# A linear-attention and SwiGLU kernel: y and the state update move ahead of the weight work in steps 6 to 11

## The chip, the cores and the metric

The kernel runs on one core of a Trainium2 chip. The metric is the device time of one execution in microseconds (us). A second figure is the span of one profiled execution, from the first to the last instruction; all times inside the kernel are counted from the start of that span.

The engines are called by short names: PE does matrix products (PEld is its weight load), ACT, DVE and POOL are three elementwise engines, and SP issues most of the DMA transfers. Each runs its own list of instructions in the order in which the program writes them, and they wait for one another through semaphores.

## The reference

The first half is an attention with a decaying state; its output becomes the input rows of a gated feed-forward block.

```python
# r, k, v: (4, 8, 768, 48); w, u: (8, 48)
for t in range(S):
    cur = einsum('bhd,bhe->bhde', u * k[t], v[t])
    y[t] = einsum('bhd,bhde->bhe', r[t], state + cur)
    state = w * state + einsum('bhd,bhe->bhde', k[t], v[t])
# x: y as (4*768, 8*48) = (3072, 384)
g = x @ w_gate                      # (384, 1536)
out = (g * sigmoid(g) * (x @ w_val)) @ w_out      # (3072, 384)
```

## The kernel before

The 768 time steps are cut into 6 chunks of 128, and with 4 batches this makes 24 units; unit i is chunk i // 4 of batch i % 4. Inside a unit the recurrence is done with matrix products: k and r are scaled by powers of w, `turn` transposes them on PE into PSUM tiles `tp`, from which ACT copies them to kT and rT (L341, L345). `scores` (L373) multiplies kT by rT into two tiles `s_ps`, and DVE's copy_predicated puts the part above the diagonal into At. `outputs` (L389) makes y of the unit: At times v and, from the second chunk on, the batch's state Z times rT, into `y_ps`, which ACT copies to xT. `update` (L415) multiplies k by v into `u_ps`; DVE adds it to Z and POOL scales Z by w.

The feed-forward work is cut into small pieces in a list `todo`, taken by `feed`. A piece of the first kind is `gate_value` (L442): twelve matmuls of 256 columns into one tile `gv`, a sigmoid on ACT and two products on DVE. Later pieces are products of a Strassen-like scheme (`four`, `project`). With a piece, `feed(1, 3)` also takes up to three ACT products that write the diagonal of At (L320). The weights come as 64-bit numbers and are rounded to 32 bits in 18 pieces by `round_weights`: three ACT passes (`w_mag` and `w_low`, L173 and L179), four DVE passes (L188, L189) and a POOL add (L216), which belongs to the piece before. After the 18 pieces the same places in the program hold four POOL subtractions of output weights (`weight_sum`).

The program's order is the engines' order: the schedule is written by hand. One loop over s (L804) runs the steps. A step s prepares unit s + 1 (POOL products, DMA loads on SP), turns unit s, does the scores of unit s - 1, and the y and state of unit s - 2. Between these stand five gaps. In steps 5 to 11 the dictionary EARLY says what a gap holds: F is a feed, R is a call of round_weights. For steps 7 to 11 the five gaps hold R, F, R, F and RF; for steps 5 and 6 the first one is empty. From step 12 on, k and r are turned by DMA and DVE instead of PE, and the gaps hold an even share of the list.

The PSUM pool `ps_a` has four buffers used in rotation. A step below 12 asks for six tiles: two `tp`, two `s_ps`, one `y_ps`, one `u_ps`. The tile `gv` has a pool of its own with two buffers.

The lines that place y and the state in the step are these:

```python
            scores(s - 1)
            if s >= LATE:
                outputs(s - 2)
                update(s - 2)
            gaps(s, 1)
...
        gaps(s, 2)
        if s - 2 >= 4 and (s < LATE or s > N):
            outputs(s - 2)
            update(s - 2)
```

Of the kernel before, what the change touches and what calls it, by code (L numbers as in the profile page):

```python
# [22 lines left out]
def fast(  # L23
# [349 lines left out]
    def scores(i):  # L373

        ps = [ps_a.tile([P, HP, P], FP32, name="s_ps", tag="a") for _ in range(2)]
        for a in range(HP):
            for e in range(2):
                rows = slice(64 * e, 64 * e + D)
                pe.matmul(  # L379
                    ps[e][:, a, :], kT[i % 2][rows, at(i, a), :], turned[i][rows, at(i, a), :],  # L380
                    start=True, stop=True, skip_group_check=True,
                )
        for e in range(2):
            dve.copy_predicated(  # L384
                At[i % 2][:].rearrange("p (a e) t -> p a e t", e=2)[:, :, e],
                mask[:].bitcast(INT32).unsqueeze(1).to_broadcast([P, HP, P]), ps[e][:],
            )

    def outputs(i):  # L389

        c, b = divmod(i, B)
        A, vl, z = At[i % 2], v_ld[i % 4], Z[b]
        rT = turned.pop(i)
        ps = ps_a.tile([P, CC, P], FP32, name="y_ps", tag="a")
        cols = [[] for _ in range(4)]
        for m in range(4 * CC):
            (cc, q), (a, s) = divmod(m, 4), divmod(m, 3)
            each = [(z[0:R2, a, 32 * s : 32 * s + 32], rT[0:R2, at(i, a), :])] if c > 0 else []  # L400
            if s < 2:
                each.append((vl[:, a, 32 * s : 32 * s + 32], A[:, 2 * a, :]))
            if s > 0:
                each.append((vl[:, a, 32 * s + 16 : 32 * s + 48], A[:, 2 * a + 1, :]))
            cols[q] += [(cc, x, n == 0, n == len(each) - 1) for n, x in enumerate(each)]
        for n in range(len(cols[0])):
            for q in range(4):
                cc, x, start, stop = cols[q][n]
                pe.matmul(  # L409
                    ps[32 * q : 32 * q + 32, cc, :], *x,  # L410
                    start=start, stop=stop, skip_group_check=True,
                )
        act.copy(xT[:, i % NX, :, :], ps[:])  # L413
# [287 lines left out]
    def gaps(s, n):  # L701

        if s not in EARLY:
            if n == 0:
                share[0] = min(-(-len(todo) // (4 - (s - 9) % 4)), 14)
            feed(share[0] // 5 + (n < share[0] % 5))
            return
        for what in EARLY[s][n]:
            if what == "R":
                if done["pool"] < NW:  # L710
                    round_weights()
                elif len(summed) < 4:
                    weight_sum()
            else:
                feed(1, 3)

    share = [0]
    BLOCKS = 12
    LATE = 12
    EARLY = {s: ("" if s < 7 else "R", "F", "R", "F", "RF") for s in range(5, 12)}  # L720
    EARLY[4] = ("R", "F", "", "F", "F")

# [81 lines left out]
    for s in range(4, N + 2):  # L804
# [11 lines left out]
        if 4 <= s - 1 < N:  # L816
            while small:
                small.popleft()()
# [3 lines that stand above are left out]
# [6 lines left out]
# [3 lines that stand above are left out]
# [22 lines left out]
@with_exitstack  # L853
def kernel(
    ctx: ExitStack,
    tc: tile.TileContext,
    *args: bass.AP,
):
    nc = tc.nc
    ctx.enter_context(tc.manual_schedule())  # L860
    flag = ctx.enter_context(tc.tile_pool(name="flag", bufs=1))
    outside = flag.tile([1, 1], INT32, name="outside")
    fast(tc, *args, outside[:])
    n = nc.values_load(outside[:], min_val=0, max_val=512)
    with tc.If(n > 0):
        general(tc, *args)
# [397 lines left out]
```

## Time and profile before

| what | value |
|---|---|
| device time, median of 3 runs | 625.29 us (624.53 to 626.14) |
| span of the profiled execution | 623.3 us |
| PE busy | 611.0 us, 98% |
| DVE, ACT, POOL busy | 358.6, 238.9, 296.9 us |
| step 6, from its y to the next: PE, DVE, ACT, POOL busy of 12.15 us | 12.15, 10.90, 11.50, 10.15 us |
| one gv group of six matmuls inside a run, start to start | about 1.3 us |
| y_ps of a unit, then u_ps, start to start | 1.56 and 0.45 us |
| granted PE clock | 0.999 |

A busy share is an average over a whole span or window. The matmuls overlap one another, so the distance between the starts of two groups says more of their cost than the duration that a line gives. An idle time is shown with the releaser, the instruction whose end let the waiting one go.

### The profile page before, as it was taken

How to read it: one execution, taken by the hardware profiler on the slowest of the kernel's cores; microseconds unless marked ns; L12 is line 12 of the kernel's file. 1: busy time of each engine (PE TensorE's matmuls, PEld its weight loads, DVE VectorE, ACT ScalarE, POOL GpSimd, SP SyncE). 2: the span in 40 equal slices, each digit the busy share in tenths (PEclk: the TensorE clock that was granted, in tenths of full speed). 3: DMA queues.
4: the chain of work that ended last, by engine and by line, in shares of the span. 5: the costliest groups of instructions: out<-in, count | busy, mean ns of one | idle time of the engine just before them, and what ended most of it. 6: DMA issues, size and time to landing. Idle time of an engine off the chain costs nothing.

```text
span 623.3 us, 13014 instructions
## 1 busy us (share of the span) xinstructions
PE 611.0 (98%) x5040; PEld 552.1 (89%) x5040; DVE 358.6 (58%) x751; ACT 238.9 (38%) x647; POOL 296.9 (48%) x350
## 2 busy tenths in 40 slices
PE   8799999999999999999999999999999999999996
PEld 7688888899888899888899888899988899988896
DVE  6888997373566574466575355574354463355460
ACT  3368785312444412344331335422243321233310
POOL 4789789935556315364452636341334211443110
PEclk9999999999999999999999999999999999999999
DMA  7989873233232213322223312221000000000001
GB/s 187 218 215 252 260 242 65 50 62 82 57 60 34 40 16 76 65 42 46 44 34 70 78 16 32 31 41 38 26 1 2 2 0 26 26 1 2 1 2 56
DMA packets 138008, 40.47 MB, mean 65 GB/s; under 512 B 128592, under 2 KB 131792, under 8 KB 137936
## 3 DMA queue, kind: packets, MB, share of 16 engines
q1 hardware_dynamic: 134480, 34.82, 26.4%
q10 hardware_dynamic: 3456, 4.72, 2.1%
q8 instruction: 42, 0.69, 0.5%
q14 instruction: 30, 0.25, 0.1%
HBM read 28.51 MB, written 4.72 MB: 53 GB/s over the span
## 4 chain that ended last, share of the span: by engine, by line
PE 90%; POOL 2%; DMA 1%; ACT 1%; DVE 1%; issue 0%; SPq 0%; ACTq 0%; POOLq 0%
PE c_b L625 25%; PE c_a L625 21%; PE o_f L519 13%; PE o_a L519 8%; PE gv L448 7%; PE o_b L519 6%; PE y_ps L409 5%; PE s_ps L379 3%; PE u_ps L424 1%; PE tp L341 1%; DMA r_ld<-in_r_dram 1%; POOL wg L216 1%; POOL wv L216 1%; POOL rk L228 0%; POOL hats L299 0%
## 5 line engine op out<-in xcount | busy, mean ns | idle before, releaser
L609 POOL TENSOR_TENSOR hT<-hT,u 128x256 f32<-128x256 f32 x60 | 47.0, 785 | 148.7 <-DVE hT L608 121.6
L632 ACT COPY u<-c_a 128x256 f32<-128x256 f32 x120 | 44.5, 371 | 85.8 <-PE c_a L625 83.3
L625 PE MATMUL c_a<-t,wv 128*128 128x256 f32 x240 | 72.1, 382 | 0.1
L625 PE MATMUL c_b<-xT,wg 128*128 128x256 f32 x240 | 71.7, 380 | 0.0
L605 ACT ACTIVATE sg<-hT 128x256 f32<-128x256 f32 x120 | 50.0, 416 | 52.5 <-DVE hT L634 33.8
L320 ACT ACTIVATE At<-ident,du 128x128 f32<-128x128 f32 x176 | 62.0, 398 | 16.0 <-DVE o_sb L533 7.2
L625 PE MATMUL c_b<-xT,s 128*128 128x256 f32 x240 | 61.7, 380 | 0.0
L639 DVE TENSOR_TENSOR u<-u,c_b 128x256 f32<-128x256 f32 x60 | 25.1, 419 | 60.5 <-PE c_b L625 55.4
L625 PEld LDWEIGHTS c_a<-t,wv 128*128 128x128 f32 x240 | 45.0, 190 | 6.8 <-ACT u L632 1.2
L625 PEld LDWEIGHTS c_b<-xT,s 128*128 128x128 f32 x240 | 45.3, 190 | 6.5
L625 PEld LDWEIGHTS c_b<-xT,wg 128*128 128x128 f32 x240 | 45.4, 190 | 5.9
L634 DVE TENSOR_TENSOR hT<-p,c_b 128x256 f32<-128x256 f32 x60 | 25.2, 420 | 41.7 <-PE c_b L625 39.1
L585 POOL TENSOR_TENSOR s<-wv,wg 128x256 f32<-128x256 f32 x24 | 17.6, 734 | 65.5 <-PE o_f L519 50.8
L384 DVE COPY_PREDICATED At<-mask,s_ps 128x512 f32<-128x512 int32 x48 | 33.0, 741 | 21.3 <-PE s_ps L379 12.4
L302 POOL TENSOR_TENSOR hats<-r_ld,rscale 128x384 f32<-128x384 f32 x20 | 20.8, 1040 | 35.3 <-DMA hats<-hats 25.2
L448 PE MATMUL gv<-xT,wg 128*128 128x256 f32 x144 | 36.7, 391 | 0.6 <-ACT xT L413 0.6
L637 DVE TENSOR_TENSOR hT<-hT,c_a 128x256 f32<-128x256 f32 x60 | 25.3, 421 | 19.5 <-PE c_a L625 18.3
L641 DVE TENSOR_TENSOR hT<-u,c_b 128x256 f32<-128x256 f32 x60 | 25.2, 421 | 19.4 <-PE c_b L625 19.2
L625 PE MATMUL c_b<-t,s 128*128 128x256 f32 x120 | 36.2, 383 | 0.0
L409 PE MATMUL y_ps<-At,v_ld 128*32 128x128 f32 x768 | 34.9, 273 | 1.3 <-DVE At L384 1.3
L625 PE MATMUL c_b<-xT,wv 128*128 128x256 f32 x120 | 35.9, 381 | 0.0
L625 PE MATMUL c_a<-t,s 128*128 128x256 f32 x120 | 35.8, 380 | 0.0
(135 smaller groups left out, 1384.3 us busy)
## 6 DMA issues: line engine op xcount, KB each, us to landing
hats<-hats SPq DMA_DIRECT2D x192, 32.0 KB, 2.0
w_bits<-in_moe_w_gate_dram SPq DMA_DIRECT2D x6, 768.0 KB, 6.4
v_ld<-in_v_dram SPq DMA_DIRECT2D x48, 96.0 KB, 3.3
w_bits<-in_moe_w_val_dram SPq DMA_DIRECT2D x6, 768.0 KB, 6.3
w_bits<-in_moe_w_out_dram SPq DMA_DIRECT2D x6, 768.0 KB, 6.7
out_dram<-o_sb ACTq DMA_DIRECT2D x24, 192.0 KB, 1.9
k_ld<-in_k_dram SPq DMA_DIRECT2D x20, 192.0 KB, 3.1
r_ld<-in_r_dram SPq DMA_DIRECT2D x20, 192.0 KB, 3.8
```

Source lines behind the costliest of these rows:

```text
L320: lambda h=h: act.activation(At[i % 2][:, h, :], ident[:], AF.Identity, scale=du[:, h : h + 1])
L384: dve.copy_predicated(At[i % 2][:].rearrange("p (a e) t -> p a e t", e=2)[:, :, e], mask[:].bitcast(INT32).unsqueeze(1).to_broadcast([P, H ...
L409: pe.matmul(ps[32 * q : 32 * q + 32, cc, :], *x, start=start, stop=stop, skip_group_check=True,)
L448: pe.matmul(gv[:, o, :].rearrange("p (i t) -> p i t", i=2), wt[:, c, P * f : P * (f + 1)], xT[:, 2 * g % NX : 2 * g % NX + 2, c, :], start ...
L519: pe.matmul(ps, lhs[:, f, :], rhs[:, f, :], start=(f == 0 and n in (0, 1, 4)), stop=(f == FH - 1), skip_group_check=True,)
L605: act.activation(x[what, f][:], h[j], AF.Sigmoid)
L609: pool.tensor_mul(h[1], h[1], x.pop(("u3", f))[:])
L625: pe.matmul(ps.rearrange("p (i t) -> p i t", i=2), lhs, rhs, start=first, stop=what not in ("p2", "p5", "p4", "p3"), skip_group_check=True,)
L632: act.copy(x[nm, f][:], ps)
L634: dve.tensor_add(h[0], x.pop(("p1", f))[:], ps)
L637: dve.tensor_mul(h[0], h[0], ps)
L641: dve.tensor_add(h[1], x.pop(("u2", f))[:], ps)
```

## The change

One constant goes from 12 to 6. In steps 6 to 11, `outputs(s - 2)` and `update(s - 2)` no longer stand behind the second and third gap (F and R), but directly behind `scores(s - 1)`. These are the units 4 to 9. On PE this means: scores, y, u and then three gate_value pieces in a row, where there was one gate_value piece between scores and y and two behind u. The xT copy on ACT, the Z additions on DVE and the Z products on POOL move with it. In step 11 the block of DMAs that begins to turn unit 12 stands behind y and u instead of ahead of them. Steps 4, 5 and those from 12 on are as they were.

```diff
     share = [0]
     BLOCKS = 12
-    LATE = 12
+    LATE = 6
     EARLY = {s: ("" if s < 7 else "R", "F", "R", "F", "RF") for s in range(5, 12)}
```

## The prediction

> **What bounds the kernel now.** I read the page first: the share of each engine, then the chain that ended last, then the timelines of PE, ACT, POOL and DVE over the six steps that the change touches (s = 6 to 11, about 53 to 131 us).
>
> ```profile
> PE 611.0 (98%) x5040; PEld 552.1 (89%) x5040; DVE 358.6 (58%) x751; ACT 238.9 (38%) x647; POOL 296.9 (48%) x350
> ```
>
> PE is busy nearly everywhere, but shares are averages. In the windows by step, the first touched step reads (span, then busy time of PE, PEld, DVE, ACT, POOL):
>
> ```profile
> 57.76:69.91 12.15, 12.15 (x149) 10.56 (x149) 10.90 (x24) 11.50 (x29) 10.15 (x10) 1.00 0.87 257
> ```
>
> PE has no hole in those 12.15 us, yet ACT, DVE and POOL are at 95%, 90% and 84%: they still round weights (calls R: three ACT passes, four DVE passes, one POOL add each). The four steps from 69.91 to 118.50 also show PE full, and from 131 to 600 us the windows have 468.8 of 468.9 us busy. So what PE loses or wins in steps 6 to 11 should reach the end undiminished.
>
> The chain of waits in order of time (start, length, what) says how step 6 was reached:
>
> ```profile
> 52.90 1.80 POOL wv L216
> 54.70 0.02 issue
> 54.73 0.93 ACT w_low L179
> 55.65 0.41 ACT w_mag L173
> 56.06 0.30 ACT sg L454
> 56.37 0.87 ACT At L320 x3
> 57.24 0.48 ACT kT L345
> 57.72 0.04 issue
> 57.76 1.75 PE y_ps L409 x56
> ```
>
> Here y of unit 4 waited for ACT's copy kT of unit 6. Not for its contents: the pool ps_a has four PSUM buffers in rotation, and a step asks for six (two tp, two s_ps, y_ps, u_ps), so y_ps always gets the buffer of the first tp of the same step, and that copy empties it. The copy was late because ACT had waited on a POOL add to reuse w_low. In PE's timeline (start, duration) that wait hardly shows:
>
> ```profile
> 54.61 1.56 PE L448 MATMUL gv<-xT,wg 128*128 128x256 f32 x6
> 56.01 1.46 PE L448 MATMUL gv<-xT,wv 128*128 128x256 f32 x6
> 57.76 0.43 PE L409 MATMUL y_ps<-rT,Z 112*32 112x128 f32 x8 [0.29 <-ACT kT L345]
> ```
>
> PE spent almost the whole delay on a gate_value call (F) that stands between scores and y. This is the point of the case.
>
> A step in steady state, PE's timeline of step 8:
>
> ```profile
> 79.27 1.56 PE L448 MATMUL gv<-xT,wg 128*128 128x256 f32 x6
> 80.67 1.46 PE L448 MATMUL gv<-xT,wv 128*128 128x256 f32 x6
> 82.06 0.43 PE L409 MATMUL y_ps<-rT,Z 112*32 112x128 f32 x8
> ...
> 83.62 0.52 PE L424 MATMUL u_ps<-v_ld,hats 128*32 128x48 f32 x32
> 84.07 1.56 PE L448 MATMUL gv<-xT,wg 128*128 128x256 f32 x6
> 85.47 1.46 PE L448 MATMUL gv<-xT,wv 128*128 128x256 f32 x6
> 86.77 1.46 PE L448 MATMUL gv<-xT,wg 128*128 128x256 f32 x6
> 88.06 1.46 PE L448 MATMUL gv<-xT,wv 128*128 128x256 f32 x6
> 89.36 0.82 PE L341 MATMUL tp<-ident,hats 128*128 128x128 f32 x6
> ```
>
> From start to start: a group of six gv matmuls inside a run takes 1.295 us, the first after smaller tiles 1.40, the last ahead of y_ps 1.39. So the lone F costs 2.79 and the two together 5.29.
>
> [...] nothing from behind y_ps ran in the 0.36 us hole at 57.40. So a matmul put ahead of an F holds the F back. [...] the granted clock is 1.00 throughout. [...] The trace shows one such buffer wait, the 0.29 us above.
>
> **The change part by part.** No instruction is added or removed. In each of steps 6 to 11 the 56 matmuls of y, the 32 of u, ACT's xT copy, DVE's two Z adds and POOL's two Z products move ahead of F, R (and F's sigmoid and two products). No DMA is issued by what moves.
>
> *Junctions on PE, a gain.* F now stands with the two others: 1.40 + 5 x 1.295 = 7.88 us against 2.79 + 5.29 = 8.08, so 0.20 less a step, 1.2 in six. Scores to y costs what scores to F does: step 12 has that order already, and there s_ps to y_ps starts 131.10 and 132.19, 1.09 us, as at 78.18 to 79.27. PE's own step becomes 0.97 (tp) + 1.09 + 1.56 + 0.45 + 7.88 = 11.95 against 12.15.
>
> *Step 6, the loss.* All that leads to kT at 57.72 lies ahead of the moved code, so y stays at 57.76. Scores end at 54.61. PE now idles 3.15 us, and F, which filled 2.79 of it, comes after u (59.78). Three F end at 59.78 + 7.88 = 67.66, where the turn of unit 7 started at 65.06: 2.59 later. This is net of the first 0.20.
>
> *Steps 7 and 8, the new bound.* y must follow kT of its own step. Behind the second F, ACT has in order: its sigmoid, three At, R (1.76), the third sigmoid, three At, kT. In step 6 that ran from 62.47 (end of gv) to 67.24, 4.77 us, plus 0.06 to y: 4.83. PE itself needs from the same point 2.59 (third F) + 0.97 + 1.09 = 4.65. So each y waits 0.18: second F ends at 65.06, y at 69.89; then 7.30 to the next second F's end and 4.83 again, 12.13 a step: y at 82.02 and 94.15.
>
> *Steps 9 to 11.* The last R of step 9 has only a POOL add, since all 18 pieces have been through ACT. ACT then needs some 2.0 us from the third F's end to kT against PE's 2.06: no wait, 11.95 each. y at 106.10 and 118.05; u ends at 120.06, two F at 125.35, where the projection's first o_a started at 123.21 before. The sum is **+2.14 us**.
>
> *The other queues.* ACT: xT's copy ahead of the sigmoid waits for y's end, but the five At products that precede it end at 59.67 and y at 59.33, so about nothing; R behind it starts 2.8 us later in step 6 because the sigmoid it follows waits for the later F, and this is what the 4.77 already holds. DVE: Z's adds stand behind the copy_predicated that ended at 60.79, when u is done, so they run about 2 us earlier; F's products and R queue behind 0.73 us. POOL: Z's product goes ahead of an R add; worked through, POOL's add of R ends at about 78.2 in step 7 and the ACT pass that reuses its buffer is due at 79.1, a margin of 0.9. PSUM of F: the third F needs the first F's products, done 1.1 us ahead. SP: loads of v wait for u, which ends at the same times as before to a few tenths; loads of k and r wait for POOL's own product, about 1 us later with a step in hand; step 11's block-moving DMAs read nothing that moved. I count these at nothing; what hides them is PE's 12 us step, and POOL works a step ahead of PE. In steps 7 and 8 the bounds are 0 (ACT comes earlier) and 1 us each (R waits on POOL or DVE); from both sides, 0.4 below and 1.6 above the sum. The 3.15 us at step 6 is bounded too: the copy hangs on a DMA of r that landed at 46.88 and a full POOL[...].
>
> **The rivals.**
> 1. *The filled wait opens and is never recovered* (forecast). 625.29 + 2.14 = 627.4; own range 626.6 to 628.4. Chance 0.52, of which 0.04 stays within the bound.
> 2. *The copy is earlier than in this one execution.* The page shows one; if kT comes 1 us sooner, step 6 loses 1.6, and the total is +1.1, 626.4. For it: the start depends on DMA; against: the three runs lie within 1.6 us. Chance 0.22, mostly no change.
> 3. *Not slower: PE's junctions decide.* If ACT's kT of step 6 is done when scores end, six gains of 0.20 remain: 624.1. It decides as soon as the copy comes before 54.7, three microseconds earlier than in the trace; what speaks for it is only that from step 7 on kT is within 0.2 us of being in time. Chance 0.10, a third of it over the bound, if more than the junctions comes free.
> 4. *ACT, DVE or POOL fall further behind.* They are 84 to 95% busy in step 6. If R waits 1 us more in steps 7 and 8[...], the total is about +3.8: 629.1. Chance 0.16.
> That the change does nothing is excluded: the order is written out by hand, and units 4 to 9 are all moved.
>
> **How the numbers follow.** The profile's own span would go from 623.3 to 625.4; the runs (624.53 to 626.14) lie 1 to 3 us above that span, so I add the sum to their median: 627.4. The bound for no change is 0.3%, 1.9 us, about what a measurement of this kernel can tell. From the cases: slower by more 0.67, within 0.30, faster 0.03. The range reaches down to case 2 with kT 1.9 us sooner and up past the middle of case 4: 625.5 to 629.5.
>
> **What would show it right or wrong.** In the changed profile y_ps of step 6 should carry about 3 us of idle time released by kT, at about 57.8; the y_ps of steps 7 and 8 some 0.2 each, those of 9 to 11 none; three F in a row of 7.9 us; steps of 12.1, then 11.95; the first o_a about 2.1 us later, and no difference after it. Wrong would be: y_ps of step 6 before 56, waits on kT of over 0.5 in later steps, a PE clock below 1, or a different length of what follows 125 us.

## The result and the profile after

The changed kernel takes 628.92 us (median of 6 runs, 628.20 to 630.11) against 625.50 us before (6 runs, 624.53 to 626.14): 1.0057 times the time before, 95% interval 1.0043 to 1.0071, so 3.4 us slower. A second set of runs on another chip gave 629.93 against 625.65, again 1.0057 (1.0041 to 1.0074); the medians themselves lie 4.3 us apart there. The prediction was 627.4, range 625.5 to 629.5, slower with a chance of 0.67.

The page of the changed kernel shows almost the same PE work in a longer span (628.4 us, 623.3 before):

```profile
PE 612.8 (98%) x5040; PEld 554.0 (88%) x5040; DVE 356.9 (57%) x751; ACT 238.7 (38%) x647; POOL 296.3 (47%) x350
```

The windows from y to y (span, busy time of PE, PEld, DVE, ACT, POOL, then the granted PE clock) say where the time went. Steps 6, 7, 9 and 10:

```profile
57.43:72.21 14.78, 14.66 (x148) 12.76 (x149) 9.14 (x20) 9.05 (x24) 9.13 (x9) 0.81 0.81 226
72.21:84.34 12.13, 12.02 (x148) 10.61 (x148) 11.15 (x24) 9.83 (x24) 10.35 (x10) 1.00 0.80 238
...
96.48:108.43 11.95, 11.95 (x148) 10.62 (x148) 9.74 (x21) 8.32 (x21) 10.17 (x10) 1.00 0.33 63
108.43:120.38 11.95, 11.95 (x150) 10.62 (x148) 5.11 (x11) 4.92 (x15) 11.64 (x9) 1.00 0.28 51
```

Steps 7, 9 and 10 take 12.13, 11.95 and 11.95 us, as forecast. Step 6 takes 14.78, and its clock is 0.81: the profile before had 1.00 there.

The chain of waits that leads to y of step 6 is nearly the old one, and y starts at nearly the old time, 57.43 (57.76 before):

```profile
52.60 1.79 POOL wv L216
54.40 0.02 issue
54.42 0.91 ACT w_low L179
55.33 0.40 ACT w_mag L173
55.73 0.30 ACT sg L454
56.04 0.87 ACT At L320 x3
56.91 0.48 ACT kT L345
57.39 0.04 issue
57.43 0.63 PE y_ps L409 x5
```

What changed is what PE does meanwhile. Its timeline of step 6, from the scores to the next turn:

```profile
53.21 1.16 PE L379 MATMUL s_ps<-rT,kT 48*128 48x128 f32 x16
57.43 0.65 PE L409 MATMUL y_ps<-rT,Z 112*32 112x128 f32 x8 [3.06 <-ACT kT L345]
...
60.42 0.87 PE L424 MATMUL u_ps<-v_ld,hats 128*32 128x48 f32 x32
61.22 2.44 PE L448 MATMUL gv<-xT,wg 128*128 128x256 f32 x6
63.49 1.46 PE L448 MATMUL gv<-xT,wv 128*128 128x256 f32 x6
...
69.97 1.04 PE L341 MATMUL tp<-ident,hats 128*128 128x128 f32 x8
```

PE waits 3.06 us for the copy that it waited 0.29 for before, since the F that lay between is now behind. The first matmuls after the hole are slow: y to u takes 2.99 us (1.56 before), u to F 0.80 (0.45), the first gv group 2.27 (1.40), together 2.65 us too long. The windows of one microsecond show why; the granted clock is the third number from the end:

```profile
55.00:56.00 1.00, 0.00 (x0) 0.00 (x0) 0.49 (x2) 1.00 (x4) 1.00 (x1) 1.00 0.91 168
56.00:57.00 1.00, 0.00 (x0) 0.00 (x0) 0.96 (x3) 1.00 (x5) 1.00 (x2) 0.60 0.95 328
57.00:58.00 1.00, 0.57 (x12) 0.54 (x16) 0.96 (x3) 1.00 (x3) 1.00 (x2) 0.50 1.05 381
...
62.00:63.00 1.00, 1.00 (x4) 0.82 (x3) 0.12 (x1) 0.00 (x0) 0.85 (x3) 0.50 1.14 197
63.00:64.00 1.00, 1.00 (x6) 0.84 (x5) 0.00 (x0) 0.00 (x0) 1.00 (x1) 0.99 0.79 156
```

A mean of 0.60 in the second window puts the fall to half at 56.2, some 1.8 us after the scores' last matmul had ended (54.4); full speed is back at 63.0. From then on everything is a shift: the first o_a, where the gates end, starts at 127.68 (123.21 before), and from there to the end it takes 500.7 us (500.1 before).

### The profile page after: what moved, and what is told of

Read it like the earlier page. It is cut to its first block, busy times and chain, and to the rows that moved or that the text cites. A ratio compares the mean times of both kernels' runs of the same rounds, so it can differ in the third digit from the quotient of the medians.

```text
span 628.4 us, 13007 instructions
## 1 busy us (share of the span) xinstructions
PE 612.8 (98%) x5040; PEld 554.0 (88%) x5040; DVE 356.9 (57%) x751; ACT 238.7 (38%) x647; POOL 296.3 (47%) x350
## 4 chain that ended last, share of the span: by engine, by line
PE 86%; POOL 3%; ACT 3%; DVE 2%; issue 1%; ACTq 0%; POOLq 0%
PE c_b L625 25%; PE c_a L625 20%; PE o_f L519 13%; PE o_a L519 8%; PE o_b L519 6%; PE y_ps L409 6%; PE gv L448 5%; PE s_ps L379 3%; PE u_ps L424 1%; ACT At L320 1%; POOL wv L216 1%; ACT w_low L179 1%; ACT w_mag L173 0%; POOL hats L299 0%; POOL rk L228 0%
## 5 line engine op out<-in xcount | busy, mean ns | idle before, releaser
L409 PE MATMUL y_ps<-At,v_ld 128*32 128x128 f32 x768 | 36.2, 279 | 1.3 <-issue 1.2
```

The costliest lines, as they stand in the source:

```text
L409: pe.matmul(ps[32 * q : 32 * q + 32, cc, :], *x, start=start, stop=stop, skip_group_check=True,)
```

## The experiments

The state of the theory after the two profiles: the copy kT of unit 6 is late for reasons that lie ahead of the changed code; F used to hide that; without it PE idles 3 us, and for a part of the runs the clock halves behind the hole. The rivals: the new order itself costs in every step, because ACT, DVE and POOL fall behind; the clock has no part; the wait only moves elsewhere when the copy is made early.

All times of before are of the same chip and set of runs as the kernel beside it. Since the profiles come to step 6 up to 2 us apart, through what happens before it, I also give the *stretch*: from the start of unit 6's turn to the first o_a in the profile. Before it is 123.21 - 52.55 = 70.66 us, in the changed kernel 127.68 - 52.25 = 75.43.

**Step 6 alone.** The kernel with the new order in step 6 and the old one in steps 7 to 11:

```diff
-            if s >= LATE:
+            if s == 6 or s >= 12:
...
-        if s - 2 >= 4 and (s < LATE or s > N):
+        if s - 2 >= 4 and (s < 12 and s != 6 or s > N):
```

> y and state move ahead in step 6 alone; steps 7 to 11 keep the old order. Theory (the wait for kT in step 6 opens a hole of 3 us that was filled before, and the PE clock halves behind it): the whole loss is here and the five other steps' gains are not, so about 3.9 us slower than before, 629.4 (2.6 for the F that comes later, 1.3 for the clock, as a mean of runs with and without a halving). Rival (ACT, DVE or POOL fall behind in steps 7 to 11 by the new order): within 0.5 us of before, 625.5.

Measured: 630.37 us against 626.08, 1.0072 (1.0059 to 1.0085), stretch 75.12. y of step 6 waits 3.34 us for kT. The clock is half for 3.4 us, from 60.06, which is 1.2 us after the hole had ended. From y to the next turn it takes 11.50 us, 1.61 more than the 9.89 at full clock (7.30 before and the 2.59 of the late F). y itself starts 5.47 us after the turn, 0.26 later than before, and 0.26 + 2.59 + 1.61 is the whole 4.46 us by which the stretch is longer. The whole loss sits in step 6; the rival of a cost in every step falls as the main cause.

**Steps 7 to 11 alone**, with the constant 7, and a second profile of the same kernel:

```diff
-    LATE = 6
+    LATE = 7
```

> The constant is 7: step 6 keeps the old order, steps 7 to 11 have the new one. Theory: no hole of 3 us, no halving; PE gains 0.20 in each of steps 9 to 11 and almost nothing in 7 and 8, where y waits about 0.2 for kT: 0.4 to 0.6 us faster than before, 625.0. Rival (the new order itself costs, in every step): 2 to 3 us slower, 628.

> A second look at the constant 7, whose runs lay between 626.1 and 628.8. Theory (without the F ahead of y, a weight piece that lands late delays kT and with it y of step 7 or 8, by an amount that differs from run to run): in a run above 627 one of these waits is 1 us or more, and it begins with a wait of ACT on w_bits. Rival (the clock differs for other reasons): the waits are 0.2 to 0.4 as in the first look, and the granted clock is lower.

Measured: 627.14 us (16 runs, 626.07 to 628.75) against 626.08, 1.0017 (1.0009 to 1.0024). This is no hole of 3 us, but neither the small gain that I expected: it is 1 us slower. The first profile (626.17 us, stretch 70.50) has waits of y for kT of 0.3 in step 6, as before, and 0.4 in step 8. The second (626.75 us, stretch 71.01) has more in step 8. Of its PE timeline, y of step 8:

```profile
80.95 0.43 PE L409 MATMUL y_ps<-rT,Z 112*32 112x128 f32 x8 [0.92 <-ACT kT L345]
```

and of its waits from 50 to 135 us (us in total, how often, the longest), those of ACT on weight pieces:

```profile
ACT w_mag L173 <- DMA w_bits<-in_moe_w_val_dram: 1.9, 1, 1.9
...
ACT w_mag L173 <- DMA w_bits<-in_moe_w_out_dram: 0.7, 1, 0.7
```

The second of these is the one ahead of y of step 8. In the first profile it is 0.18 us, so it grew by 0.52, and so did the wait of y, from 0.40 to 0.92. In the kernel with the constant 9 (below), where step 8 has the old order, ACT waits 0.73 for the same piece and y does not wait at all. So here a late weight piece does reach y, and the old order hid it. Neither profile is of a run above 627, so the runs up to 628.75 stay without one. That they too are late weight pieces is argued, not shown: four of the six runs above 627.5 have mean clocks of 0.994 to 0.996, and only one of the ten others has, so the rival of the clock is open for them, and with it the cause of most of the 1 us.

**Filling the hole.** The changed kernel with matmuls of no use between scores and y of step 6. The first version had 24 calls:

```diff
+    def fill(n):
+        ps = ps_f.tile([P, 2, 2 * P], FP32, name="fill", tag="gv")
+        for _ in range(n):
+            pe.matmul(ps[:, 0, 0:P], ident[:], ident[:], start=True, stop=True)
...
+            if s == 6:
+                fill(24)
             if s >= LATE:
```

> The changed kernel, with 24 matmuls of the identity by itself (2.7 us, results unused) between scores and y of step 6, in a gv tile of their own. Theory (hole plus halved clock): the hole is filled by work without use, y starts at the same time, but the clock stays at 1.00, so only the 2.1 us of the prediction's sum are left: 627.6. Rival (the clock has no part in the loss, the 3.4 us are waits): as the changed kernel, 628.9, or later if the fill delays y. Rival (clock halving is not caused by this hole): the halving stays, clock 0.993 to 0.996.

Measured: 630.93 us against 626.08, 1.0073 (1.0060 to 1.0086), stretch 75.79. It was a miss in size: the profile counts 48 passes for the 24 calls on this 32-bit data, two for one; they took 5.55 us and held y back to 61.23. (So the twelve matmuls of a gate_value, the 56 of y and the 32 of u are passes too, of 6, 28 and 16 calls.) The clock stayed at 1.00 (54 to 75 us), but nothing follows on the loss. The second version had 12 calls:

```diff
-                fill(24)
+                fill(12)
```

> The changed kernel with half the fill: 12 calls, 24 passes on PE, 2.8 us by the 5.55 us that 48 passes took (results unused), between scores and y of step 6. Theory (of the loss of 3.4 us about 2.2 are the hole, the rest is the halved clock behind it): y starts when kT is there, the clock stays at 1.00 in 54 to 65 us, and about 2.2 us of loss are left: 0.35% slower than before. Rival (the clock has no part): 0.55 to 0.6% slower, as the changed kernel.

Measured: 628.58 us against 626.12, 1.0040 (1.0025 to 1.0055), stretch 73.94. Of its PE timeline, the fill and y, then a window over both:

```profile
55.48 2.95 PE L268 MATMUL fill<-ident 128*128 128x128 f32 x24
59.75 0.43 PE L414 MATMUL y_ps<-rT,Z 112*32 112x128 f32 x8 [1.32 <-ACT kT L350]
```

```profile
56.00:60.00 4.00, 2.68 (x31) 2.48 (x34) 2.95 (x7) 3.74 (x9) 4.00 (x4) 1.00 0.82 221
```

In this profile kT was later still (ACT waited 3.2 us for a weight piece), so 1.32 us of the hole stayed open, yet the clock is 1.00, and stays there to 66 us. y starts 6.33 us after the turn (5.21 before), 1.12 later, and with the prediction's 2.14 this makes 3.26 of the 3.28 by which the stretch is longer. So with the clock held, the sum is right. The changed kernel measured 1.0057 and the filled one 1.0040; the intervals overlap, so the totals alone don't prove the 1 us between them. The profiles show 2.65 us of slow matmuls in the one and none in the other, each for one execution. The mean clocks of all runs point the same way: on average 0.998 in the nine runs of the filled kernel, 0.998 in those of before beside it, and 0.996 and 0.994 in the two sets of the changed kernel.

**The changed kernel again**, on the chip of the last set:

```diff
     LATE = 6
```

> The changed kernel once more, beside the others on one chip. Theory (a hole of about 3 us in step 6, then a clock halved for part of the runs): 0.5 to 0.6% slower than before, and from the turn of unit 6 to the first o_a about 74 to 75.5 us, against 70.7 in the profile of before; in a profile without a halving about 73.

Measured: 629.93 us against 625.65, 1.0057 (1.0041 to 1.0074), stretch 75.27. In the profile (the run at 631.54 us) y waits for the copy:

```profile
59.33 0.66 PE L409 MATMUL y_ps<-rT,Z 112*32 112x128 f32 x8 [2.93 <-ACT kT L345]
```

The clock is half from 58.0 to 64.9. Of the other five runs, the one with a mean clock of 1.000 took 628.26, those with 0.993 took 630.47 and 630.89. The run without a loss of clock is 2.6 us above the median before; of the runs in the first set, that with 0.999 is 2.7 above. This is the hole. The profiled run is 3.3 us above the 628.26. In its profile 2.6 us of this are slow matmuls behind the hole (y to the next turn takes 12.50 us, against 9.89). But not all of it belongs to the change: the clock was also half from 27.3 to 30.7, ahead of every changed step. Two windows of this profile, in the order of the columns above:

```profile
27.00:28.00 1.00, 1.00 (x12) 0.94 (x12) 0.83 (x2) 0.00 (x0) 0.92 (x2) 0.65 1.02 377
28.00:29.00 1.00, 1.00 (x18) 0.78 (x20) 0.61 (x1) 0.00 (x0) 0.58 (x1) 0.50 1.09 329
```

The groups that this spell slows (scores, u and scores again, up to y) take 4.61 us from start to start; in the first profile of the changed kernel they take 3.81, so the spell costs 0.8. The profile of the kernel with the constant 9 (below) has the same spell, 27.2 to 30.6, with a mean clock of 0.995, and no hole in step 6. So a low mean clock of a run without a profile doesn't say where the clock was lost.

**Making the copy early.** The changed kernel, with the last R of step 5 moved behind the turn of unit 6, so that ACT copies kT first:

```diff
+    EARLY[5] = ("", "F", "R", "F", "F")
+    EARLY[6] = ("R", "F", "R", "F", "RF")
```

> The changed kernel, with the last R of step 5 moved behind the turn of unit 6 (first gap of step 6), so that ACT copies kT of unit 6 before that R and not behind it. Theory (the late copy alone makes the hole): y of step 6 follows scores with under 0.3 us of wait, the clock stays at 1.00, and the gains of the junctions and the 0.36 us that y waited before come free: about 1 us faster than before, 624.5. Rival (the new order costs by itself): 627 to 629, with the wait only moved to another place.

Measured: 629.61 us against 626.08, 1.0055 (1.0034 to 1.0076), stretch 73.53. y of step 6 follows at once, and step 7 has the hole. From its waits, 50 to 72 us (us in total, how often, the longest):

```profile
PE y_ps L409 <- ACT kT L345: 2.4, 1, 2.4
ACT w_mag L173 <- DMA w_bits<-in_moe_w_val_dram: 2.2, 1, 2.2
```

The rival was right: the wait moved. R also issues the load of a later weight piece; on SP's queue that load now stood behind the loads of k and r of unit 9, which wait for POOL, went out at 60.55 and was missed by 2.2 us. The clock halved here too, from 70.5 to 73.9, and y of step 7 to the next turn takes 11.51 us, again 1.6 more than 9.89. The mended form sends these loads of k and r after the R:

```diff
-            if s + 3 < N:
+            if s + 3 < N and s != 6:
                 load(s + 3)
...
         gaps(s, 0)
+        if s == 6:
+            load(s + 3)
```

> As the kernel with the R of step 5 moved behind the turn of unit 6, and the loads of k and r of unit 9 moved behind this R too, so that the weight load that belongs to R is issued before them, at about 57.5 us and not at 60.6. Theory (in the first form that weight piece came 2.2 us late because its load stood behind loads that wait for POOL): no hole in step 6 nor in step 7, clock 1.00, about 1 us faster than before, 0.15%. Rival (ACT and POOL are too full there for kT of unit 7 to be in time): y of step 7 waits 1 us or more and the total is no better than before.

Measured: 626.03 us against 626.12, 0.9994 (0.9983 to 1.0004), stretch 69.67. Its chain of waits through step 6 holds PE alone:

```profile
51.83 1.29 PE gv L448 x6
53.12 0.87 PE tp L341 x8
53.99 1.09 PE s_ps L379 x16
55.09 1.68 PE y_ps L409 x56
56.77 0.34 PE u_ps L424 x32
57.10 3.00 PE gv L448 x13
```

The 3.4 us are gone, with the new order of y in all six steps: the median of 14 runs is that of before. (The profile is of the fastest of them, 624.60 us.) This settles the cause: the order costs nothing by itself, the late copy that it uncovers does. The control, both moves with the old order:

```diff
-    LATE = 6
+    LATE = 12
```

> The control of the version that makes kT of unit 6 early: its two moves (the R of step 5 behind the turn of unit 6, the loads of k and r of unit 9 behind this R) with the old constant 12, so the old order of y. Theory (the new order is worth 0.2 us a step wherever kT is in time, the early copy takes away the 0.36 us of wait): from the turn of unit 6 to the first o_a 70.3 us, 0.6 us longer than the 69.67 with the constant 6; in the total about 0.3 us faster than before, not to be told from it. Rival (the gain of that version came from the moves alone): 69.7 us as well.

Measured: 625.13 us against 625.65, 0.9991 (0.9984 to 0.9999), stretch 122.80 - 52.51 = 70.29. The new order is thus worth 0.62 us when the copy is in time, by one profile of each kernel. In the totals neither version can be told from before by the bound of 0.3%, nor one from the other: I have no version that clearly beats both kernels.

**Gains of the late steps.** The constant 9:

```diff
-    LATE = 6
+    LATE = 9
```

> The constant is 9: only steps 9 to 11 have the new order. Theory (the new order gains 0.20 us a step wherever kT is in time, and steps 7 and 8, where ACT still rounds weights, are what made the constant 7 slower): 0.6 us faster than before, 0.1%. Rival (the new order costs in every step): slower by 0.5 us or more.

Measured: 626.14 us against 626.12, 1.0002 (0.9990 to 1.0013), stretch 70.05. No difference that can be measured, where I expected 0.6 us. In the profile the part from the turn of unit 9 to the first o_a is 33.47 us (33.85 before): a gain of 0.38, since y of step 9 waits 0.2 for kT behind the last R of step 8. The rest of the shorter stretch is y of step 6, which starts 4.99 us after the turn here and 5.21 before. The size was off, and below what the totals can show.

**Moving more R.** The last R of steps 5 to 10 behind the next turn, with the loads of k and r behind it:

```diff
-    EARLY = {s: ("" if s < 7 else "R", "F", "R", "F", "RF") for s in range(5, 12)}
+    EARLY = {s: ("RR", "F", "R", "F", "F") for s in range(7, 12)}
+    EARLY[5] = ("", "F", "R", "F", "F")
+    EARLY[6] = ("R", "F", "R", "F", "F")
+    EARLY[11] = ("RR", "F", "R", "F", "RF")
...
-            if s + 3 < N:
+            if s + 3 < N and not 6 <= s <= 10:
...
+        if 6 <= s <= 10:
+            load(s + 3)
```

> The constant 6, and in steps 5 to 10 the R of the last gap moved behind the next step's turn, with the loads of k and r of these steps behind it. Theory (y of steps 7 to 9 waits about 0.2 us each for kT because ACT does an R between the last two F; with that R behind kT the wait goes): from the turn of unit 6 to the first o_a 69.1 us, 0.6 less than with the one R moved, and about 1.5 us faster than before, 0.25%. Rival (two R at the start of a step make the copy_predicated, the sigmoids or the weight pieces late): new waits of y or gv of 0.5 us or more, no faster than before.

Measured: 627.84 us against 625.65, 1.0029 (1.0019 to 1.0039), stretch 72.50. The waits of y on kT are gone, and others are there. From its waits, 60 to 105 us:

```profile
POOL Z L437 <- DVE Z L436: 5.1, 3, 1.7
DVE sg L455 <- ACT sg L454: 2.9, 4, 1.3
PE gv L448 <- DVE hT L456: 2.7, 3, 0.9
```

With two R at the head of a step ACT and DVE come late to the first F, and the third F waits 0.9 us, in three steps, for the gv buffer of the first. The rival was right.

## Why the prediction was right, and what it mis-sized

*Junctions.* Right: three F in a row from 74.23 to 82.10 take 7.87 us (7.88 forecast), scores to y 1.09, PE's own step 11.95.

*Step 6.* Right in mechanism and place: y stayed at 57.4, the hole is 3.06 us (3.13 counted from start to start, as the forecast counted its 3.15), and without the clock's part the next turn would be 2.59 later relative to y, as forecast. The cause of the late copy was only half right. I read one chain, which ends on a POOL add. In seven of the eight other profiles that keep this R in its place, ACT had first waited 1.1 to 3.2 us for a weight piece by DMA (1.6 in the changed kernel); whether the piece or the POOL add ends last differs from run to run.

*Steps 7 and 8.* Right to 0.02 us: y waits 0.19 and 0.18 (0.18), steps 12.13 and 12.14 (12.13). *Steps 9 to 11:* 0.19 at y of step 9, which the sum had included, though the list of signs says none there; then none, and 11.95 each.

*The sum.* From y of step 6 to the first o_a it takes 70.25 us, 65.45 before. Of these 4.80 us, 2.65 are the slow matmuls, and 2.15 are left for the sum's +2.14. The runs without a lost clock (+2.6 and +2.7) and the filled kernel (+2.5) are near it; the medians of the two sets are +3.4 and +4.3. So the total is right by the width of its range, not by its sum: 628.92 lies above the forecast case's own 626.6 to 628.4 and next to the fourth rival's 629.1, and a clock below 1, one of the signs of being wrong, did come. The step that failed is the price of the clock: the forecast took it as nothing. That a hole of 3.15 us would leave the clock at 1.00 was an assumption of mine, shown by no trace: in the profile before, the longest wait of PE behind its first matmul is 1.19 us (at 17.95, with the clock at 1.00). The trace of the changed kernel decides otherwise: half speed began 1.8 us into the idle time and cost 2.65 us of slow matmuls in the profiled run. In the medians I estimate 0.8 and 1.7 us, from +3.4 and +4.3 less the 2.6 of a run without a lost clock; some of that may be the earlier spell.

*The rivals.* The second (an earlier copy; its 1 us was an estimate of mine) came in neither profile: y of step 6 starts 5.21, 5.18 and 5.06 us after the turn of unit 6 before, in the changed kernel and in its second profile. The third (junctions decide) was too high even where the copy is in time: 0.62 us and not 1.2, since steps 7 to 9 keep their waits of 0.2. The fourth, R waiting 1 us more in steps 7 and 8, is seen in no profile of the changed kernel, but with the constant 7 one profile has 0.9 us in step 8.

*The other queues.* Rightly nothing for SP, POOL and DVE: PE waits for none of them in steps 6 to 11. That SP's order can matter was shown only where an R was moved past the loads of k and r.

## What to carry to other kernels

An engine that never idles may be busy because of a filler: before moving work, look for the wait that is short in the trace only because other work stands ahead of it, and price the move by the whole delay of what it waits for. Where the hole is on TensorE, add the clock to this price: all four profiled holes of 2.4 to 3.3 us in the steps studied here were followed by half speed, and the runs give no length below which it is safe. And when a call is moved, follow its DMA in the queue too: the first repair here failed through one load that came to stand behind two others.

## What the runs showed of the hardware

The PE clock fell to half 1.8 us (changed kernel) and 1.6 us (its second profile) after the last matmul had ended, in idle times of 3.06 and 2.93 us. It stayed there for 6.8 and 6.9 us, though PE was busy again after 1.2 and 1.3 us of it. In two other kernels (the new order in step 6 alone, and the first form of the early copy) holes of 3.34 and 2.37 us were followed by half speed for 3.4 us, beginning 1.2 and 0.9 us after the hole had ended. The spell at 27 us, seen in two profiles, also lasted 3.4 us. A hole of 1.32 us behind the fill left the clock at 1.00, and so did the 2.84 us that PE waits for its first matmul in the kernel before.

The length of a single hole thus doesn't decide it: 2.37 us came with half speed, 2.84 us at the start did not. What decides was not tested. Behind the holes in step 6 and 7 the spells of 3.4 us cost 1.6 us and the long ones 2.6, and two runs of the changed kernel kept a mean clock of 0.999 and 1.000. With the earlier spell, which cost 0.8, this is my reading of why the runs of the changed kernel spread over 1.9 and 3.3 us in the two sets; only two of the twelve have a profile.
